# Pooled attention scores of two heads as one product over 128 rows, with zero-padded keys

## The chip, the cores and the metric

The kernel runs on one core of a Trainium2 chip. The metric is device time in microseconds (us) of one execution, from launch to end; less is better. A profile of one execution adds the span, which is the time from that execution's first instruction to its last, and the clock that TensorE was granted in each stretch: it has two levels, 2.4 GHz (shown as 1.00) and 1.2 GHz (0.50).

The engines are named as in the profile: PE is TensorE's matrix product, PEld its loading of weights (the stationary operand), DVE is VectorE, ACT is ScalarE, POOL is GpSimd, and SP is the engine that issues the DMAs.

## The reference, cut to what matters

Attention over 8 batches and 8 heads of 576 positions with 64 features, in two branches that are added, and then a gated feed-forward layer on all 4608 tokens:

```python
B, H, S, D = 8, 8, 576, 64; factor = 4; Sd = S // factor      # Sd = 144
q_d, k_d, v_d = (mean over 4 neighbouring positions)          # the pooled branch
out_d = sm_attn(q_d, k_d, v_d)                                # scores are 144 x 144 for each head
out_up = np.repeat(out_d, factor, axis=2)
mask = np.abs(pos[:, None] - pos[None, :]) < factor           # the local branch
out_local = softmax(where(mask, scale * q @ k.T, -1e9)) @ v
x = (out_up + out_local) as 4608 tokens x 512
gate = 1 / (1 + exp(-(x @ w_gate)));  val = x @ w_val         # 512 -> 1536
return (gate * val) @ w_out                                   # 1536 -> 512
```

The change is in the scores of the pooled branch, q_d @ k_d.T of each head.

## The kernel before, in words

**Units.** Attention is worked in 32 units. A unit is one batch and a pair of heads: head 0's 64 features lie on partitions 0 to 63, head 1's on partitions 64 to 127. Units 0 to 3 are batch 0, units 4 to 7 batch 1, and so on. Each unit is a dictionary of small steps (`unit_steps`, L412 on), and a table of positions says where in the program each step is written; the compile-time scheduler then fixes the order of the instructions on each engine from its own estimate of times. Each engine runs its own queue in order.

**The pooled branch of a unit.** `prep2` (L452) sums four neighbouring positions of q and k. They come as one tile `qkd` of 128 x 1152 from DRAM. `sum4` (L381) adds pairs in place on POOL (L383), then adds the two halves (L385) into the tile `qks` of 128 x 288: 144 columns of q sums and 144 of k sums, for both heads, one head on each half of the partitions. There is one buffer for `qks`. `s_down(h)` (L501) makes the scores of head h in one PSUM bank: two products of 64 rows (this head's partitions) x 72 query columns as weights, against 144 key columns, one for each half of the queries (qb). Then come the row maxima of both (L511, DVE, 72 x 288 read), their scaling (L512, ACT) and two exponentials with their sums (L514, ACT) into the tile `e`. `s_down(0)` is step d0, `s_down(1)` step d1; they are placed apart in the table. `norm_down` scales `e` into `ad`, `t_down` transposes it on PE (`adt`), and `av_down` multiplies by the pooled v (`od`): there `vdblk` holds both heads' v as a block-diagonal matrix with zeros beside it, so its products run over 128 rows.

**All products are issued at L394**, in `product`. One product of fp32 operands is two PE instructions in the profile (and two weight loads); one of fp16 is one. The weights' shape stands in the profile as rows*columns, "64*72" or "128*128", ahead of the shape of the moving operand.

**The local branch** uses `s` (scores of 10 blocks, block-diagonal q in `qblk`), `t` (softmax), `at` (transposes) and `x` (the product with v). For units 4 on, `s`, `sd`, `at`, `adt`, `od` and `x` share two PSUM banks by turns (L446, tile tag "att").

**The feed-forward part** goes by 9 chunks of 512 tokens and 12 blocks of 128 hidden features: `moe_gate` (products `pg`, 12 instructions), `moe_val` (`pv`, 12) and `moe_out` (`po`, 12), all fp16 in split high and low parts, 128*128 weights against 512 columns. During the first part of the program the weights arrive from DRAM, their maxima are taken (`hmx`), and they are converted (L205 to L215) on ACT, DVE and POOL. From position C1 on (L771 to L780), the steps of the later units are written between the blocks of `pg`, `pv` and `po` of chunks 1 to 8.

**At the start,** zeros are written into the block-diagonal tiles (`zeroed`, L98); `awake` products of a zero tile are put between the steps of the first units on PE.

Of the kernel before, what the change touches and what calls it, by code (L numbers as in the profile page):

```python
# [10 lines left out]
F32 = mybir.dt.float32  # L11
I32 = mybir.dt.int32
AF = mybir.ActivationFunctionType
ALU = mybir.AluOpType
AX = mybir.AxisListType
# [5 lines left out]
P = 128  # L21
# [9 lines left out]
SD = S // 4  # L31
QM = SD // 2
# [12 lines left out]
NWT = 1 + 2 * NPC  # L45
NST = 5
NPLAIN = 8
QKSCALE = 1.0 / 8
WAHEAD = 1
MAHEAD = 3  # L50
# [7 lines left out]
def attention_moe(ctx, tc, qk, qkd, v, vd, wg, wv, wo, mask, out):  # L58
    nc = tc.nc
# [3 lines left out]
    wk = ctx.enter_context(tc.tile_pool(name="wk", bufs=2))  # L63
# [34 lines left out]
    def zeroed(eng, shape, dtype, name):  # L98
        t = cp.tile(shape, dtype, tag=name, name=name)
        eng.memset(t, 0.0)  # L100
        return t

    def borrowed(eng, i, n):
        t = borrow(i, n * P)
        eng.memset(t, 0.0)
        return t.rearrange("p (a b) -> p a b", a=n)

    qblk = [zeroed(nc.vector, [P, 2 * NJ, P], F32, f"qblk{i}") for i in range(2)]
    vplain = [borrowed(nc.vector, 0, NBLK), borrowed(nc.gpsimd, 0, NBLK)]
    vdblk = [zeroed(nc.gpsimd, [P, NKC, P], F32, f"vdblk{i}") for i in range(2)]  # L110
    ad = zeroed(nc.gpsimd, [QM, 2, NKC, 2, WIN], F32, "ad")
    vblk = cp.tile([P, 2, NBLK, P], F16, tag="vblk", name="vblk")
    flat = {id(vblk): vblk.rearrange("p t b c -> p (t b c)").bitcast(F32)}
# [229 lines left out]
    qkraw, qkdraw, vdraw = {}, {}, {}  # L343
# [37 lines left out]
    def sum4(out, x, eng=nc.gpsimd):  # L381

        nc.gpsimd.tensor_tensor(out=x[:, :, 0:2], in0=x[:, :, 0:2], in1=x[:, :, 2:4], op=ALU.add)  # L383
        for ps, o in out:
            eng.tensor_tensor(out=o, in0=x[ps, :, 0], in1=x[ps, :, 1], op=ALU.add)  # L385

    ALL = slice(0, P)
    HALVES = [slice(0, 64), slice(64, P)]

    def product(o, w, x, first=True, last=True):  # L390

        pairs = ((0, 0), (0, 1), (1, 0)) if len(w) == 2 else ((0, 0),)
        for i, (a, c) in enumerate(pairs):
            nc.tensor.matmul(o, w[a], x[c], start=first and i == 0, stop=last and i == len(pairs) - 1)  # L394
# [4 lines left out]
    def own(t, u):  # L399
        owner[id(t)] = u  # L400

    def mine(t, u):
        assert owner[id(t)] == u, (owner[id(t)], u)

    def zero(*tiles):

        for t in tiles:
            nc.gpsimd.memset(flat[id(t)], 0.0)
            own(t, "zero")

    def unit_steps(u):
        b, hp = divmod(u, NPAIR)  # L412
        s = st[u] = {}
        NQ = 2 * NJ * R
        plain = u < NPLAIN
        AD = ad
# [8 lines left out]
        QB, VDB = qblk[u % 2], vdblk[u % 2]  # L425
# [3 lines left out]
        def take(t):  # L429
            if t is vblk and u in (NPAIR, NPLAIN):  # L430
                assert owner[id(t)] == "zero", (u, owner[id(t)])
            own(t, u)
# [13 lines left out]
        def bank(own, name):  # L446

            if u < NPAIR:
                return ps_o.tile([P, 512], F32, tag=own, name=name)
            return ps_a.tile([P, 512], F32, tag="att", name=name)  # L450

        def prep2():  # L452
            t = qkdraw[u]
            sums = wk.tile([P, 2, SD], F32, tag="qks", name=f"qks_{u}", bufs=1)
            sum4([(ALL, sums.rearrange("p a b -> p (a b)"))], t.rearrange("p (g f) -> p g f", f=4))
            s["qd"], s["kd"] = sums[:, 0], sums[:, 1]

        def s_local(j0, j1):
            mine(QB, u)
# [4 lines left out]
            if j0 == 0:  # L464
                s["t"] = wk.tile([P, NJ, 2 * WIN], F32, tag="t", name=f"t_{u}")
            nc.vector.scalar_tensor_tensor(  # L466
                out=s["t"][:, j0:j1, :], in0=pt[:, : n * 2 * WIN].rearrange("p (a b) -> p a b", a=n),
                scalar=QKSCALE, in1=mk[:, j0:j1, :], op0=ALU.mult, op1=ALU.add)

# [26 lines left out]
        def vdsum():  # L496
            take(VDB)
            x = vdraw[u].rearrange("p a b f -> p (a b) f")
            sum4([(ps, VDB[ps, :, ps]) for ps in HALVES], x, nc.vector if u in T["vd"] else nc.gpsimd)

        def s_down(h):  # L501
            pt = bank(f"o{h}", f"sd_{u}_{h}")
            hs = slice(h * 64, h * 64 + 64)
            for qb in range(2):
                o, rows = pt[:QM, qb * SD : (qb + 1) * SD], slice(qb * QM, (qb + 1) * QM)
                product(o, [s["qd"][hs, rows]], [s["kd"][hs]])
            if h == 0:
                s["e"] = wk.tile([QM, 2, 2, SD], F32, tag="e", name=f"e_{u}", bufs=1)
                s["sme"] = wk.tile([QM, 4], F32, tag="sme", name=f"sme_{u}")
            mx = wk.tile([QM, 2], F32, tag="mxd", name=f"mxd_{u}_{h}")  # L510
            nc.vector.tensor_reduce(mx, pt[:QM, : 2 * SD].rearrange("p (q c) -> p q c", q=2), axis=AX.X, op=ALU.max)  # L511
            nc.scalar.activation(mx, mx, AF.Copy, scale=-QKSCALE / 16)  # L512
            for qb in range(2):
                nc.scalar.activation(s["e"][:, qb, h, :], pt[:QM, qb * SD : (qb + 1) * SD], AF.Exp,  # L514
                                     bias=mx[:, qb : qb + 1], scale=QKSCALE / 16,
                                     accum_out=s["sme"][:, 2 * qb + h : 2 * qb + h + 1])

        def norm_down():
# [51 lines left out]
        def av_local(i0, i1):  # L570
            mine(VT, u)
            pt = bank("gate" if i0 == 0 else "val", f"x_{u}_{i0}")
            for i in range(i0, i1):
                product(pt[:, (i - i0) * R : (i - i0 + 1) * R], [x[:, i] for x in VBp], [x[:, i] for x in s["at"]])
            if i0 == 0:
                s["xs"] = wk.tile([P, S], F32, tag="xs", name=f"xs_{u}", bufs=1)
            t0, t1 = i0 * R, min(i1 * R, S)
            g0, g1 = t0 // 4, t1 // 4
            o = s["xs"][:, t0:t1].rearrange("p (g f) -> p g f", f=4)
            x = pt[:, : t1 - t0].rearrange("p (g f) -> p g f", f=4)  # L580
            y = s["od"][:, g0:g1].unsqueeze(2).to_broadcast([P, g1 - g0, 4])
            if plain:
                nc.vector.scalar_tensor_tensor(out=o, in0=x, scalar=sxb[:, b : b + 1], in1=y, op0=ALU.mult, op1=ALU.add)
            else:
                nc.vector.tensor_tensor(out=o, in0=x, in1=y, op=ALU.add)

        def xsplit():
            for c, o, i, n in segs_of_batch(b):
                x = xtile(c)
                src = s["xs"][:, i : i + n]  # L590
                nc.scalar.copy(x[:, hp, 0, o : o + n], src)  # L591
                eng = nc.vector if u in T["xd"] else nc.gpsimd
                eng.tensor_tensor(out=x[:, hp, 1, o : o + n], in0=src, in1=x[:, hp, 0, o : o + n], op=ALU.subtract)  # L593
            del st[u]
            done.add(u)

        return dict(
            prep0=lambda: None, prep1=prep1, prep2=prep2, s0=p1, s1=p2, sm=p2b,
            d0=lambda: s_down(0), d1=lambda: s_down(1), dn=norm_down,
            vd=vdsum, v=plain_v if plain else vsplit,  # L600
            a0=lambda: t_local(0, 3), a1=lambda: t_local(3, 5), at=t_down, od=av_down,
            x=lambda: (av_local(0, 8), av_local(8, 10), xsplit()),
# [7 lines left out]
    def moe_gate(c, fc):  # L610
        assert ("g", fc) in done
        assert all(u in done for u in range(min(NU, -(-(c + 1) * CH // S) * NPAIR))), (c, fc)
        x = xT[c]
        pt = ps_o.tile([P, CH], F32, tag="gate", name=f"pg_{c}_{fc}")
        for k in range(4):
            product(pt, [wg16[:, fc, a, k, :] for a in range(2)], [x[:, k, e, :] for e in range(2)], k == 0, k == 3)
        t = wk.tile([P, CH], F32, tag="tanh", name=f"tanh_{c}_{fc}")
        for b, o, n in segs_of_chunk(c):
            nc.scalar.activation(t[:, o : o + n], pt[:, o : o + n], AF.Tanh, scale=tsc[:, b, fc : fc + 1])  # L619
        return t  # L620
# [50 lines left out]
    def add(pos, f):  # L671
        steps.setdefault(pos, []).append(f)
# [31 lines left out]
    def base(u):  # L704
        if u < NPAIR:
            return 1 + u * T["pro"]
        if u < 2 * NPAIR:
            return T[f"u{u}"]
        if u < 3 * NPAIR:
            return C1 - T["b8"] + (u - 2 * NPAIR) * T["s8"]  # L710
        return C1 + T["b12"] + (u - 3 * NPAIR) * T["s12"]

    def offset(u, k):
        if u < NPAIR:
            return ALONE[k] * T["al"]
        return AMONG[k] * (T["am"] if u < 2 * NPAIR else 1)

    for u in range(NU):
        b, hp = divmod(u, NPAIR)
# [28 lines left out]
    add(T["z"], lambda: zero(vblk))  # L748
    add(base(NPLAIN - 1) + offset(NPLAIN - 1, "x") + 1, lambda: zero(vblk))

# [21 lines left out]
    for c in range(1, NCHUNK):  # L772
        for fc in range(NFC):
            t = moe_gate(c, fc)
# [86 lines left out]
```

## Time and profile before

| what | value |
|---|---|
| median of three runs | 1137.96 us (1137.18 to 1144.3) |
| the profiled execution, its own time | 1139.3 us |
| its span, first to last instruction | 1137.5 us |
| time outside the span | 1.8 us |
| mean granted TensorE clock | 0.968 |
| PE busy | 1097.7 us (96%) |
| DVE, ACT, POOL busy | 566.8, 488.1, 335.5 us |

A busy time is the sum of the durations of an engine's instructions without overlap. Durations of products on PE contain a tail that overlaps the next one, so the cost of a product in a stream is read from the distance between starts. In a timeline row the first number is the start in the span, the second the time from the first start to the last end of the merged instructions. "Idle before <- X" names what released an engine after a wait. The chain is the work that ended last, followed back from the end.

### The profile page before, as it was taken

The numbers are of one execution on the slowest core, as the hardware profiler recorded it, in microseconds if no ns is written. First come the engines' busy times: TensorE is split into PE (matmuls) and PEld (weight loads), VectorE is DVE, ScalarE is ACT, GpSimd is POOL, SyncE is SP. The second block draws the span as 40 slices with busy tenths as digits, with TensorE's granted clock in tenths as the row PEclk, the third lists the DMA queues.
The fourth block names the chain that finished last, engine by engine and source line by source line (L and its number), as shares of the span: only waits on it lengthen the run. The fifth ranks groups of instructions, "written<-read, shape, count | busy, mean of one in ns | idle before, by whom it ended". The sixth has DMA issues, their size and how long they took to land.

```text
span 1137.5 us, 16128 instructions
## 1 busy us (share of the span) xinstructions
PE 1097.7 (96%) x6319; PEld 603.6 (53%) x6319; DVE 566.8 (50%) x1048; ACT 488.1 (43%) x1112; POOL 335.5 (29%) x352
## 2 busy tenths in 40 slices
PE   7879879999999999999999999999999999999998
PEld 5854534555555555555555555555555554444443
DVE  7789989854445544444444444444444432122121
ACT  6635666533445444444445443544454332112112
POOL 6335646222223333333333332333243210000000
PEclk9758889999999999999999999999999999999999
DMA  9887766332213222132223121311121000000001
GB/s 361 330 311 258 252 210 216 118 100 86 70 47 131 60 65 70 59 111 74 69 69 106 61 65 56 119 59 54 48 94 36 1 1 37 1 1 37 1 1 37
DMA packets 31900, 110.33 MB, mean 97 GB/s; under 512 B 3536, under 2 KB 3664, under 8 KB 31824
## 3 DMA queue, kind: packets, MB, share of 16 engines
q1 hardware_dynamic: 31824, 109.30, 28.7%
q8 instruction: 50, 0.82, 0.3%
q14 instruction: 26, 0.21, 0.1%
HBM read 99.84 MB, written 9.44 MB: 96 GB/s over the span
## 4 chain that ended last, share of the span: by engine, by line
PE 86%; DVE 7%; DMA 2%; ACT 2%; issue 1%; POOL 1%; SPq 0%; DVEq 0%; ACTq 0%; POOLq 0%
PE po L394 24%; PE pg L394 23%; PE pv L394 23%; PE s L394 5%; PE x L394 3%; PE sd L394 3%; PE od L394 2%; PE at L546 1%; PE adt L556 1%; DVE wrg L207 1%; DMA v<-in_v_dram 1%; DVE vdblk L385 1%; DVE hmx L152 0%; DMA wo3c<-in_wo_dram 0%; DVE wrv L207 0%
## 5 line engine op out<-in xcount | busy, mean ns | idle before, releaser
L394 PE MATMUL pg<-xT,wg 128*128 128x512 f16 x1296 | 311.9, 383 | 6.7 <-ACT wg L214 3.5
L394 PE MATMUL pv<-xT,wv 128*128 128x512 f16 x1296 | 311.8, 381 | 0.1
L394 PE MATMUL po<-g,wo 128*128 128x512 f16 x1188 | 280.8, 379 | 0.0
L394 PEld LDWEIGHTS <-wg 128*128 128x128 f16 x1296 | 125.8, 99 | 152.0 <-issue 7.7
L394 PEld LDWEIGHTS <-wo 128*128 128x128 f16 x1296 | 124.7, 99 | 153.1 <-issue 8.2
L394 PEld LDWEIGHTS <-wv 128*128 128x128 f16 x1296 | 125.6, 99 | 141.0 <-issue 4.9
L627 DVE SCALAR_TENSOR_TENSOR tanh<-tanh,pv 128x512 f32<-128x512 f32 x108 | 73.8, 683 | 203.6 <-PE pv L394 199.3
L619 ACT ACTIVATE tanh<-pg,tsc 128x512 f32<-128x512 f32 (+7 forms) x192 | 87.0, 497 | 163.7 <-PE pg L394 163.7
L635 ACT ACTIVATE g<-tanh,gs 128x512 f16<-128x512 f32 x99 | 71.5, 723 | 149.6 <-DVE tanh L627 148.4
L636 DVE SCALAR_TENSOR_TENSOR g<-tanh,gs,g 128x512 f16<-128x512 f32 x99 | 88.6, 895 | 52.4 <-ACT g L635 51.9
L478 POOL TENSOR_TENSOR t<-t,mx 128x640 f32<-128x640 f32 x32 | 44.0, 1376 | 186.5 <-DVE mx L477 186.5
L394 PEld LDWEIGHTS s<-qk,qblk 128*128 128x128 f32 x600 | 77.9, 198 | 10.6 <-DVE hx L191 1.9
L394 PE MATMUL s<-qk,qblk 128*128 128x64 f32 x600 | 77.1, 279 | 2.6 <-DVE hx L191 1.4
L593 POOL TENSOR_TENSOR xT<-xs,xT 128x384 f16<-128x384 f32 (+7 forms) x58 | 53.1, 928 | 74.1 <-ACT xT L591 73.7
L488 POOL TENSOR_TENSOR t<-t,sm 128x640 f32<-128x640 f32 x28 | 36.8, 1316 | 96.0 <-DVE sm L486 94.6
L484 DVE TENSOR_REDUCE sm<-t 128x10 f32<-128x640 f32 x32 | 26.1, 817 | 66.1 <-ACT t L479 66.0
L156 ACT ACTIVATE vblk<-v,svb 64x640 f16<-64x640 f32 x48 | 39.7, 827 | 34.6 <-PE x L394 32.9
L466 DVE SCALAR_TENSOR_TENSOR t<-s,mk 128x384 f32<-128x384 f32 x64 | 31.0, 486 | 41.9 <-PE s L394 41.8
L438 ACT COPY qblk<-qk 64x580 f32<-64x580 f32 x60 | 40.5, 676 | 23.2 <-DMA qk<-in_qk_dram 19.5
L157 DVE SCALAR_TENSOR_TENSOR vblk<-v,svb,vblk 64x640 f16<-64x640 f32 x48 | 47.3, 985 | 3.2 <-ACT vblk L156 1.6
L512 ACT ACTIVATE mxd<-mxd 72x2 f32<-72x2 f32 x64 | 13.0, 203 | 83.5 <-DVE mxd L511 83.2
L383 POOL TENSOR_TENSOR qkd<-qkd 128x576 f32<-128x576 f32 x29 | 40.1, 1382 | 28.9 <-DMA qkd<-in_qkd_dram 28.5
(292 smaller groups left out, 1180.3 us busy)
## 6 DMA issues: line engine op xcount, KB each, us to landing
qk<-in_qk_dram SPq DMA_DIRECT2D x30, 610.0 KB, 3.8
qkd<-in_qkd_dram SPq DMA_DIRECT2D x29, 576.0 KB, 3.8
vd<-in_vd_dram SPq DMA_DIRECT2D x29, 384.0 KB, 3.5
v<-in_v_dram SPq DMA_DIRECT2D x32, 320.0 KB, 3.0
out_dram<-osb SPq DMA_DIRECT2D x16, 512.0 KB, 3.1
wo<-in_qk_dram SPq DMA_DIRECT2D x2, 610.0 KB, 10.5
wo<-in_qkd_dram SPq DMA_DIRECT2D x2, 576.0 KB, 9.3
out_dram<-osb SPq DMA_DIRECT2D x4, 256.0 KB, 2.3
```

The costliest lines, as they stand in the source:

```text
L156: nc.scalar.activation(hi, src, AF.Copy, scale=sc)
L157: nc.vector.scalar_tensor_tensor(out=lo, in0=src, scalar=sc, in1=hi, op0=ALU.mult, op1=ALU.subtract)
L383: nc.gpsimd.tensor_tensor(out=x[:, :, 0:2], in0=x[:, :, 0:2], in1=x[:, :, 2:4], op=ALU.add)
L394: nc.tensor.matmul(o, w[a], x[c], start=first and i == 0, stop=last and i == len(pairs) - 1)
L438: nc.scalar.copy(QB[ps, :, ps.start : ps.start + R], q_[ps])
L478: nc.gpsimd.tensor_tensor(out=t, in0=t, in1=mx.unsqueeze(2).to_broadcast([P, NBLK, WIN]), op=ALU.subtract)
L488: eng.tensor_tensor(out=t, in0=t, in1=sm.unsqueeze(2).to_broadcast([P, NBLK, WIN]), op=ALU.mult)
L593: eng.tensor_tensor(out=x[:, hp, 1, o : o + n], in0=src, in1=x[:, hp, 0, o : o + n], op=ALU.subtract)
L619: nc.scalar.activation(t[:, o : o + n], pt[:, o : o + n], AF.Tanh, scale=tsc[:, b, fc : fc + 1])
L627: nc.vector.scalar_tensor_tensor(out=t, in0=t, scalar=1.0, in1=pt, op0=ALU.add, op1=ALU.mult)
L635: nc.scalar.activation(g[:, 0], t, AF.Copy, scale=gs[:, fc : fc + 1])
L636: nc.vector.scalar_tensor_tensor(out=g[:, 1], in0=t, scalar=gs[:, fc : fc + 1], in1=g[:, 0], op0=ALU.mult, op1=ALU.subtract)
```

## The change

The pooled k of the two heads now goes into a tile `kdblk` of 128 x 2 x 144 that was zeroed at the start: head 0's sums fill partitions 0 to 63 of its first 144 columns, head 1's fill partitions 64 to 127 of the second 144, and the other two quarters stay zero. There are two such tiles, used by turns. One product of 128 rows x 72 query columns (both heads' q) against these 288 columns gives the scores of both heads for half of the queries. So `s_down` is called for a half of the queries instead of for a head, and makes one product of 288 columns where it made two of 144; the maxima, the exponentials and `e` keep their sizes and counts. `sum4` on POOL writes its second sum in three pieces instead of one: q (128 x 144) and k of each head (64 x 144 each). `qks` now holds q alone.

```diff
+NKD = 2
...
+    kdblk = [zeroed(nc.vector, [P, 2, SD], F32, f"kdblk{i}") for i in range(NKD)]
...
-        for ps, o in out:
-            eng.tensor_tensor(out=o, in0=x[ps, :, 0], in1=x[ps, :, 1], op=ALU.add)
+        for ps, o, g in out:
+            eng.tensor_tensor(out=o, in0=x[ps, g, 0], in1=x[ps, g, 1], op=ALU.add)
...
         def prep2():
-            t = qkdraw[u]
-            sums = wk.tile([P, 2, SD], F32, tag="qks", name=f"qks_{u}", bufs=1)
-            sum4([(ALL, sums.rearrange("p a b -> p (a b)"))], t.rearrange("p (g f) -> p g f", f=4))
-            s["qd"], s["kd"] = sums[:, 0], sums[:, 1]
+            x = qkdraw[u].rearrange("p (g f) -> p g f", f=4)
+            s["qd"] = wk.tile([P, SD], F32, tag="qks", name=f"qks_{u}", bufs=1)
+            s["kd"] = kdblk[u % len(kdblk)]
+            own(s["kd"], u)
+            sum4([(ALL, s["qd"], slice(0, SD))] + [(ps, s["kd"][ps, h], slice(SD, 2 * SD)) for h, ps in enumerate(HALVES)], x)
...
-        def s_down(h):
-            pt = bank(f"o{h}", f"sd_{u}_{h}")
-            hs = slice(h * 64, h * 64 + 64)
-            for qb in range(2):
-                o, rows = pt[:QM, qb * SD : (qb + 1) * SD], slice(qb * QM, (qb + 1) * QM)
-                product(o, [s["qd"][hs, rows]], [s["kd"][hs]])
-            if h == 0:
+        def s_down(qb):
+            mine(s["kd"], u)
+            pt = bank(f"o{qb}", f"sd_{u}_{qb}")
+            product(pt[:QM, : 2 * SD], [s["qd"][:, qb * QM : (qb + 1) * QM]], [s["kd"].rearrange("p h c -> p (h c)")])
+            if qb == 0:
...
-            for qb in range(2):
-                nc.scalar.activation(s["e"][:, qb, h, :], pt[:QM, qb * SD : (qb + 1) * SD], AF.Exp,
-                                     bias=mx[:, qb : qb + 1], scale=QKSCALE / 16,
+            for h in range(2):
+                nc.scalar.activation(s["e"][:, qb, h, :], pt[:QM, h * SD : (h + 1) * SD], AF.Exp,
+                                     bias=mx[:, h : h + 1], scale=QKSCALE / 16,
```

The scheduler's order changes with it. Three places follow. A name such as sd_31_1 is the tile of unit 31 and step d1 (the last number is only a counter), "72x144 x2" two products with an output of 72 x 144, and po_6_3 is a product of chunk 6 into its fourth output quarter; line numbers after the change are two or three higher.

The first place is PE in the middle of the program, at step d1 of unit 31, among the products of chunk 6; first before, then now:

```order
L394 MATMUL po_6_3_8139<-g_6_6_8510,wo16_111 128x512
L394 MATMUL sd_31_1_8203<-qks_31_7946 72x144 x2
L394 LDWEIGHTS wo16_111
L394 MATMUL po_6_3_8139<-g_6_6_8510,wo16_111 128x512
L394 LDWEIGHTS wo16_111
L394 MATMUL po_6_3_8139<-g_6_6_8510,wo16_111 128x512
L394 MATMUL od_30_8223<-adt16_30_8184,vdblk0_118 128x144 x3
```

```order
L396 MATMUL po_6_3_8144<-g_6_6_8514,wo16_111 128x512
L396 MATMUL sd_31_1_8208<-kdblk1_124,qks_31_7950 72x288
L396 LDWEIGHTS wo16_111
L396 MATMUL po_6_3_8144<-g_6_6_8514,wo16_111 128x512
L396 LDWEIGHTS wo16_111
L396 MATMUL po_6_3_8144<-g_6_6_8514,wo16_111 128x512
L396 LDWEIGHTS wg16_109
```

The two products of 144 columns have become one of 288 at the same place between `po` products, and od_30 stands a few products later.

The second place is PE near the start, where the pooled scores of unit 3 (sd_3) stood among the local products of units 0 to 2; first before, then now:

```order
L546 MATMUL at_0_0_280<-ident_103,t_0_178 128x128 x3
L394 MATMUL sd_3_0_614<-qks_3_468 72x144 x2
L394 MATMUL sd_3_1_631<-qks_3_468 72x144 x2
L130 MATMUL mxt1_266<-mxg1_270,ones_125 128x1
L546 MATMUL at_0_3_307<-ident_103,t_0_178 128x128 x2
L394 MATMUL x_0_0_447<-at16_0_284,wg16_109 128x58 x6
L556 MATMUL adt_2_582<-ident_103,ad_122 128x72 x6
L394 MATMUL s_2_0_368<-wo16_111,qblk0_112 128x64 x6
```

```order
L396 MATMUL s_2_3_389<-wo16_111,qblk0_112 128x64 x4
L396 MATMUL x_0_0_453<-at16_0_290,wg16_109 128x58 x2
L396 MATMUL x_0_8_464<-at16_0_290,wg16_109 128x58 x2
L396 MATMUL od_1_519<-adt16_1_451,vdblk1_120 128x144 x3
L547 MATMUL at_1_0_407<-ident_103,t_1_250 128x128 x3
L557 MATMUL adt_2_588<-ident_103,ad_126 128x72 x4
L547 MATMUL at_1_3_431<-ident_103,t_1_250 128x128 x2
L557 MATMUL adt_2_588<-ident_103,ad_126 128x72
L396 MATMUL sd_3_0_620<-kdblk1_124,qks_3_474 72x288
L396 MATMUL sd_3_1_636<-kdblk1_124,qks_3_474 72x288
```

sd_3 now stands behind s_2, x_0, od_1 and at_1 (and before the products x_1), where it stood ahead of all of them.

The third place is POOL at units 9 and 10; first before, then now:

```order
L385 TENSOR_TENSOR qks_9_2218<-qkd9_2105 128x288
L531 TENSOR_TENSOR ad_122<-e_8_2187,sme_8_2188 72x2x3x48 x2
L383 TENSOR_TENSOR qkd10_2223<-qkd10_2223 128x288x2
L478 TENSOR_TENSOR t_9_2258<-t_9_2258,mx_9_2283 128x640
L385 TENSOR_TENSOR qks_10_2367<-qkd10_2223 128x288
```

```order
L387 TENSOR_TENSOR qks_9_2223<-qkd9_2111 128x144
L385 TENSOR_TENSOR qkd10_2230<-qkd10_2230 128x288x2
L532 TENSOR_TENSOR ad_126<-e_8_2192,sme_8_2193 72x2x3x48 x2
L387 TENSOR_TENSOR kdblk0_122<-qkd10_2230 64x144 x2
L481 TENSOR_TENSOR t_9_2264<-t_9_2264,mx_9_2289 128x640
L387 TENSOR_TENSOR qks_10_2372<-qkd10_2230 128x144
```

The two pieces of k stand ahead of POOL's work on t_9, and only the q piece, which writes the single `qks` buffer, stands where the whole sum stood.

## Rows read from the trace of the kernel before

**Rows 1.** Stretches: length, busy us of PE, PEld, DVE, ACT, POOL; clock, DMA share, GB/s.

```profile
0.00:80.00 80.00, 63.20 (x370) 52.90 (x370) 61.01 (x126) 43.38 (x116) 36.52 (x45) 0.74 0.88 332
80.00:200.00 120.00, 102.95 (x486) 52.80 (x484) 114.57 (x202) 73.97 (x145) 69.98 (x48) 0.89 0.73 238
200.00:225.00 25.00, 24.49 (x127) 13.26 (x128) 22.01 (x38) 13.09 (x27) 6.96 (x8) 0.93 0.40 130
225.00:937.00 712.00, 711.08 (x4433) 396.02 (x4432) 329.63 (x628) 314.48 (x751) 221.26 (x252) 1.00 0.22 68
937.00:1137.50 200.50, 195.97 (x908) 88.65 (x906) 39.63 (x56) 43.18 (x78) 0.78 (x1) 1.00 0.04 16
```

**Rows 2.** The chain from 225 us to the end, by line.

```profile
by line: PE po L394 28.3%; PE pg L394 27.3%; PE pv L394 27.3%; PE s L394 5.5%; PE sd L394 3.3%; PE x L394 2.4%; PE od L394 2.1%; PE at L546 1.5%; PE adt L556 1.0%; PE mxt L130 0.2%; DVE xs L585 0.1%; DVE vblk L157 0.1%; DVE tsc L308 0.1%; A
```

**Rows 3.** Instructions of tile sd between 225 and 937 us: min/median/max ns.

```profile
L394 PE MATMUL sd<-qks x192: 282/283/340, 242.6 to 908.0; 64*72 64x144 f32 x192
```

**Rows 4.** Timeline of PE around one pooled-score step: start, us, what, count.

```profile
906.38 1.24 PE L394 MATMUL po<-g,wo 128*128 128x512 f16 x5
907.55 0.71 PE L394 MATMUL sd<-qks 64*72 64x144 f32 x4
908.19 0.60 PE L394 MATMUL po<-g,wo 128*128 128x512 f16 x2
908.63 0.90 PE L394 MATMUL od<-adt,vdblk 128*128 128x144 f32 x6
909.37 0.38 PE L394 MATMUL pg<-xT,wg 128*128 128x512 f16 x1
```

**Rows 5.** Timeline of PE around products with one weight column, and with one row.

```profile
815.22 0.81 PE L394 MATMUL pv<-xT,wv 128*128 128x512 f16 x3
815.87 0.27 PE L125 MATMUL mxt<-ident,vm 128*1 128x128 f32 x1
815.98 0.81 PE L394 MATMUL po<-g,wo 128*128 128x512 f16 x3
...
157.23 0.59 PE L394 MATMUL pv<-xT,wv 128*128 128x512 f16 x2
157.75 0.38 PE L130 MATMUL mxt<-mxg,ones 1*128 1x1 f32 x2
```

**Rows 6.** Timeline of PE near the start, units 0 to 4.

```profile
30.86 1.25 PE L394 MATMUL sd<-qks 64*72 64x144 f32 x8
...
43.71 1.13 PE L546 MATMUL at<-ident,t 128*128 128x128 f32 x5
...
50.10 0.90 PE L394 MATMUL od<-adt,vdblk 128*128 128x144 f32 x6
...
75.03 1.23 PE L394 MATMUL sd<-qks 64*72 64x144 f32 x4
```

**Rows 7.** Clock in the stretches of the first and last row of rows 6.

```profile
30.00:32.00 2.00, 2.00 (x12) 1.33 (x11) 1.17 (x5) 1.94 (x9) 0.00 (x0) 0.50 1.01 408
75.00:77.00 2.00, 1.26 (x5) 0.79 (x4) 2.00 (x5) 0.77 (x1) 0.00 (x0) 0.50 0.93 313
```

**Rows 8.** Sums at L385 between 225 and 937 us: min/median/max ns.

```profile
L385 POOL TENSOR_TENSOR vdblk<-vd x42: 522/530/984, 303.8 to 883.2; 64x192 f32<-64x192 f32 x42
...
L385 POOL TENSOR_TENSOR qks<-qkd x23: 700/707/1598, 251.3 to 879.2; 128x288 f32<-128x288 f32 x23
```

**Rows 9.** POOL's waits, 225 to 937 us: total us, times, longest.

```profile
POOL qks L385 <- PE sd L394: 75.5, 22, 8.7
```

**Rows 10.** Timeline of DVE: the last large memset, the first v, unit 3's output.

```profile
3.89 1.12 DVE L105 MEMSET wg<- 128x1280 f32 x1 [0.21 <-issue]
...
8.82 0.82 DVE L152 TENSOR_REDUCE vm<-v 128x1 f32<-128x640 f32 x1 [3.79 <-DMA v<-in_v_dram]
...
71.72 0.70 DVE L583 SCALAR_TENSOR_TENSOR xs<-x,sxb,od 128x464 f32<-128x464 f32 x1 [3.65 <-PE x L394]
```

**Rows 11.** PE's longest wait from 200 us to the end: total us, times, longest.

```profile
PE x L394 <- ACT e L514: 2.4, 1, 2.4
```

More of the change, by code (lines that the diff above doesn't have):

```diff
@@ L498, in vdsum @@
             x = vdraw[u].rearrange("p a b f -> p (a b) f")
-            sum4([(ps, VDB[ps, :, ps]) for ps in HALVES], x, nc.vector if u in T["vd"] else nc.gpsimd)
-        def s_down(h):
-            pt = bank(f"o{h}", f"sd_{u}_{h}")
-            hs = slice(h * 64, h * 64 + 64)
-            for qb in range(2):
-                o, rows = pt[:QM, qb * SD : (qb + 1) * SD], slice(qb * QM, (qb + 1) * QM)
-                product(o, [s["qd"][hs, rows]], [s["kd"][hs]])
-            if h == 0:
+            sum4([(ps, VDB[ps, :, ps], slice(None)) for ps in HALVES], x, nc.vector if u in T["vd"] else nc.gpsimd)
+        def s_down(qb):
[3 more added lines that the diff above has]
+            if qb == 0:
                 s["e"] = wk.tile([QM, 2, 2, SD], F32, tag="e", name=f"e_{u}", bufs=1)
                 s["sme"] = wk.tile([QM, 4], F32, tag="sme", name=f"sme_{u}")
-            mx = wk.tile([QM, 2], F32, tag="mxd", name=f"mxd_{u}_{h}")
-            nc.vector.tensor_reduce(mx, pt[:QM, : 2 * SD].rearrange("p (q c) -> p q c", q=2), axis=AX.X, op=ALU.max)
+            mx = wk.tile([QM, 2], F32, tag="mxd", name=f"mxd_{u}_{qb}")
+            nc.vector.tensor_reduce(mx, pt[:QM, : 2 * SD].rearrange("p (h c) -> p h c", h=2), axis=AX.X, op=ALU.max)
             nc.scalar.activation(mx, mx, AF.Copy, scale=-QKSCALE / 16)
-            for qb in range(2):
-                nc.scalar.activation(s["e"][:, qb, h, :], pt[:QM, qb * SD : (qb + 1) * SD], AF.Exp,
-                                     bias=mx[:, qb : qb + 1], scale=QKSCALE / 16,
+            for h in range(2):
+                nc.scalar.activation(s["e"][:, qb, h, :], pt[:QM, h * SD : (h + 1) * SD], AF.Exp,
+                                     bias=mx[:, h : h + 1], scale=QKSCALE / 16,
                                      accum_out=s["sme"][:, 2 * qb + h : 2 * qb + h + 1])
```

## The prediction

> **What bounds the kernel now.** I read the stretches first, then the chain, then the timeline of PE around one pooled-score step. The stretches show three stages [rows 1]. Up to 200 us PE is not the bound: in the 120 us from 80 to 200, DVE is busy for 114.57 us and PE for 102.95, at a mean granted clock of 0.89. From 200 us on PE is full, and from 225 to 937 us it is busy for 711.08 of 712 us at the full 2.4 GHz, while DVE, ACT and POOL have 329.63, 314.48 and 221.26 us of work there. So in that stretch a microsecond less on PE ends the kernel a microsecond earlier, and nothing that the other engines gain or lose in it counts until it makes PE wait. The chain from 225 us on says the same: it is PE almost throughout, and the pooled scores (sd) hold 3.3% of its 912.5 us, 30 us [rows 2]. Units 8 to 31 fall into this stretch: 192 sd instructions, four to a step, so 48 steps [rows 3].
>
> One step's true cost stands in the timeline [rows 4]. A product of 512 columns takes 0.65 / 3 = 0.217 us from start to start (pv, the first two rows of [rows 5]). Five of them from 906.38 should give PE to sd at 907.46; sd starts at 907.55. That is 0.09 us of gap at the entry. The four sd instructions hold PE from 907.55 to 908.19, 0.64 us. The od products have the same 144 columns in fp32, but 128 rows, and stand close: six from 908.63 to 909.37, 0.123 us each. At that pace four sd instructions would take 0.49. So a step holds PE for 0.73 us, and 0.24 of that is gap: 0.09 ahead of it, 0.15 inside it and behind it. The od group right behind has none.
>
> **The change part by part.** *The products.* The same number of columns passes: four instructions of 144 before, two of 288 now. At od's pace a step takes 2 x 0.246 = 0.49 us. The question is whether the gaps go too. Two things set sd apart from od: 64 rows instead of 128, and 72 weight columns instead of 128. The trace separates them [rows 5]. A product with 128 rows and one weight column (mxt<-ident,vm) follows three pv at 815.87, just when they are done, and the next po starts 0.11 us later: no gap on either side. A product with one row and 128 weight columns (mxt<-mxg,ones) starts 0.52 us after the first of two pv that need 0.43: the same 0.09 of gap as sd. So the gap goes with the rows, and with 128 rows I expect none. Each step saves 0.24 us (0.25 if the rounding of the rows falls the other way), and 48 steps save 11.5 to 12.0; I take 11.7. If the gaps stayed whole, the step would cost 0.73 as now and the saving is zero; that is the lower end.
>
> The Trainium skill, "TensorEngine Tiling (Array Packing)", section "Key Properties", says that changing the tiling mode drains TensorE. The trace agrees with it, with 0.09 us at a switch to few rows, and by that rule too the change removes both switches of a step.
>
> *What is given up.* Heads on different halves of the rows can run side by side, and the trace shows it once: at 30.86 both steps of unit 3 stand together, and their eight instructions take 1.25 us, while at 75.03 four of unit 4 alone take 1.23 [rows 6], both at 1.2 GHz [rows 7]. With 128 rows that is over: four instructions of 288 columns at half clock are 2 x 0.98 = 1.96 us, 0.7 more, for unit 3, and about half of that for unit 0, whose two steps also stand together, at full clock. From unit 8 on the two steps of a unit stand apart, four instructions at a time, so nothing is lost there.
>
> The Trainium skill, "TensorE: Matmul & The Clock Gate", section "Part 3: Packing small matmuls — row/col tiling", speaks against this change: it advises to keep small-row products in distinct row groups, since they run concurrently. The row at 30.86 agrees, but the steps that decide the end never stand together, so by that rule only the 1 us of units 0 and 3 would be lost.
>
> *POOL's sums.* One sum of 128x288 (0.707 us) becomes one of 128x144 and two of 64x144; a 64x192 one takes 0.530 [rows 8]. A piece of 144 columns lies between half of the whole sum, 0.35, and the whole, 0.71; I take 0.44, by the 64x192 row less a quarter of its columns and some fixed part. Three make 1.3 us: 0.6 more per unit, between 0.35 and 1.4. It can't be a gain, since the three pieces cover the same columns. From 225 us on that is 24 x 0.6 = 14 us more on an engine with 490 us to spare there. Does a step wait for it? Today it is POOL that waits for PE: 75.5 us in 22 waits for sd to free the single buffer of qks [rows 9]. In the new order only the q piece stands behind that wait, so what follows it is shorter than now (0.44 against 0.71). If the cover failed, PE would wait 0.6 us in each of 24 units, 14 us, all of the gain.
>
> *Maxima and exponentials* keep their shapes and counts: nothing. *Memsets:* two of 128x288 on DVE, under 0.3 us each by the 1.12 us of 128x1280, lie in the 3.79 us in which DVE waits for the first v [rows 10]: nothing.
>
> *The first 225 us.* PE has slack here, so its savings (12 steps that stand alone) don't count by themselves. POOL's 0.6 us more in 8 units is 4.8 us at most if each held up a full DVE; the lost pairing is 1 us. On the other side, PE reaches s_2 earlier, because sd_3 and most of adt_2 no longer stand ahead of it: 1.25 us and some more at half clock. And x waits 2.4 us for an exponential at about 200 us [rows 11], of which the earlier place of the last maxima of unit 7 may save a part. I take zero for this stretch, with 4.5 us either way.
>
> *Sum.* The profiled execution took 1139.3 us, 1.8 of it outside the span; 1139.3 - 11.7 = 1127.6. It was 1.3 above the median of the runs, so against the median: 1137.96 - 11.7 = 1126.3. The 200 us after 937 us have no sd and don't change.
>
> **The rivals.** *The gaps stay*, because they belong to a narrow fp32 weight load and not to the rows. For it: the load keeps 72 columns and fp32. Against it: the one-column fp32 product without a gap. Then the time is 1138, and with half of the gaps 1132.
>
> *The start gives part of it back.* The scheduler has rearranged every engine there. If DVE's full stretch ends 4.5 to 11 us later, the time is 1131 to 1137.
>
> *The start costs more than the products gain: slower.* The place is unit 3. DVE waits 3.65 us for x_3 and adds its od at 71.72 [rows 10], and the conversion of the weights queues behind that addition. The sd_3 products move from 30.86 to behind at_1, which ends at 44.8 [rows 6], 14 us later. In the trace od_3 follows sd_3 by 50.10 - 30.86 = 19.2 us, so it would come at about 64, still 7 us ahead of its use. If the steps between (maxima, exponentials, scaling, transposes, each behind other work on its engine) take longer than that, the excess moves the rest of the program. From 11.7 us of excess on the kernel is slower; 23 us of it, three times the spare time, give 1149.
>
> *The start gains:* if x_0, x_1 and the conversions behind them all move up, up to 5 us or more go as well: 1121.
>
> **How the numbers follow.** The forecast, gaps gone and the start within 4.5 us: 0.80, from 1122 to 1131. Gaps that stay in large part: 0.06. The start gives back 4.5 to 11: 0.08. Slower: 0.03. The start gains more: 0.03. I predict 1126.3. The range for 8 times in 10, taking in the bounds of the start, is 1121.5 to 1131.5. About 1% is what a measurement can tell from no change; 1% faster is 1126.6, just beside my forecast. So half of the 0.80 and a little more lies on that side, and the gaining start: faster 0.52. Of the slower rival some 0.02 reaches 1149; the rest, 0.46, is within 1%.
>
> **What would show it.** Right: sd stands as 128*72 with 288 columns, two instructions a step, about 0.49 us from the first start to the next product; the product ahead of it keeps 0.217; the share of sd in the chain after 225 us falls from 30 to about 23 us; PE is still full there; the pure stretch of pg, pv and po starts about 11.7 us earlier. The start is right if PE's full stretch begins at 200 us again. Wrong: a step of 0.7 us (gaps stay), PE waits for POOL's sums (cover gone), or PE's full stretch beginning more than 5 us from 200 us.

## The result and the profile after

Four runs of the changed kernel have a median of 1126.56 us (1125.82 to 1131.24); four runs of the kernel before have 1137.67. The measured ratio is 0.9891, with a 95% interval from 0.9864 to 0.9917; the medians alone give 0.9902, which lies inside it. So the change gains 11.1 us by the medians, and between 9.4 and 15.5 us by the interval; 1126.3 us was predicted. The profiled execution took 1126.46 us, its span is 1124.7 us, at a mean granted clock of 0.972.

The stretches of the changed kernel, with the columns of [rows 1]:

```profile
0.00:80.00 80.00, 62.32 (x350) 52.05 (x350) 60.23 (x125) 42.05 (x110) 39.34 (x56) 0.74 0.86 324
80.00:200.00 120.00, 98.55 (x475) 49.59 (x476) 114.08 (x207) 75.08 (x153) 68.77 (x55) 0.93 0.72 246
200.00:225.00 25.00, 25.00 (x136) 13.64 (x134) 22.86 (x36) 13.16 (x25) 10.60 (x11) 0.96 0.33 120
225.00:937.00 712.00, 710.23 (x4386) 393.93 (x4385) 332.99 (x630) 315.76 (x755) 238.01 (x296) 1.00 0.21 68
937.00:1124.70 187.70, 183.12 (x849) 82.81 (x847) 37.56 (x54) 40.65 (x73) 0.00 (x0) 1.00 0.05 17
```

Nothing in the fourth row looks faster: PE is full, as in [rows 1], at the same clock. The gain appears as work that has moved forward, out of the last stretch, which is 187.70 us long instead of 200.50: the last step of sd starts at 894.86 us, where it started at 907.55 [rows 4]. In such a stage PE's busy time says nothing about whether its work is well packed; the distances between starts do. POOL's busy time in the fourth row has grown by 16.8 us.

The chain from 225 us on, by line (to set beside [rows 2]):

```profile
by line: PE po L396 28.0%; PE pg L396 27.5%; PE pv L396 27.4%; PE s L396 5.5%; PE sd L396 2.6%; PE x L396 2.4%; PE od L396 2.0%; PE at L547 1.5%; PE adt L557 1.0%; DVE vblk L159 0.4%; DMA v<-in_v_dram 0.3%; ACT vblk L158 0.2%; PE mxt L132 0
```

The share of sd is 2.6% of 899.7 us, 23.4 us, where it was 30.

One pooled-score step in the timeline of PE (to set beside [rows 4]; start, us, what, count):

```profile
576.14 2.11 PE L396 MATMUL pg<-xT,wg 128*128 128x512 f16 x9
578.09 0.65 PE L396 MATMUL sd<-kdblk,qks 128*72 128x288 f32 x2
578.57 2.54 PE L396 MATMUL pv<-xT,wv 128*128 128x512 f16 x11
```

Nine pg products from 576.14 at 0.216 us end their turn at 578.08; sd starts at 578.09, so there is no gap at the entry. The pv behind it starts 0.48 us later (0.49 and 0.50 us at two other steps). A step of the kernel before held PE for 0.73 us.

PE's waits of the changed kernel from 200 us to the end (total us, times, longest):

```profile
PE at L547 <- DVE t L469: 0.7, 1, 0.7
PE s L396 <- DVE t L469: 0.6, 1, 0.6
PE x L396 <- DVE xs L586: 0.4, 1, 0.4
```

No wait is for POOL's sums. The 2.4 us of [rows 11] is not in this list because that wait now ends at 197.20 us, ahead of the window, and has become 1.29 us; its row stands further down.

The sums of one unit on POOL, by shape (min/median/max ns; to set beside [rows 8]):

```profile
L387 POOL TENSOR_TENSOR qks<-qkd x29: 439/447/1353, 8.6 to 867.6; 128x144 f32<-128x144 f32 x29
...
L387 POOL TENSOR_TENSOR kdblk<-qkd x58: 432/446/2187, 9.0 to 847.6; 64x144 f32<-64x144 f32 x58
```

### The profile page after: what moved, and what is told of

Same layout as the page of the kernel before. It is cut to its first block, busy times and chain, and to the rows that moved or that the text cites. A ratio compares the mean times of both kernels' runs of the same rounds, so it can differ in the third digit from the quotient of the medians.

```text
span 1124.7 us, 15921 instructions
## 1 busy us (share of the span) xinstructions
PE 1079.2 (96%) x6191; PEld 592.0 (53%) x6191; DVE 567.7 (50%) x1050; ACT 486.7 (43%) x1112; POOL 356.7 (32%) x416
## 4 chain that ended last, share of the span: by engine, by line
PE 85%; DVE 8%; ACT 2%; DMA 2%; issue 2%; POOL 1%; DVEq 0%; POOLq 0%; SPq 0%; ACTq 0%
PE po L396 24%; PE pg L396 23%; PE pv L396 23%; PE s L396 5%; PE x L396 3%; PE sd L396 2%; PE od L396 2%; PE at L547 1%; PE adt L557 1%; DVE vdblk L387 1%; DVE hmx L154 1%; DVE wrg L210 1%; DMA wg6c<-in_wg_dram 1%; DVE wrv L209 0%; DVE wrg L209 0%
## 5 line engine op out<-in xcount | busy, mean ns | idle before, releaser
L515 ACT ACTIVATE e<-sd,mxd 72x144 f32<-72x144 f32 x128 | 47.0, 370 | 2.4
```

What stands on the lines that cost most here:

```text
L515: nc.scalar.activation(s["e"][:, qb, h, :], pt[:QM, h * SD : (h + 1) * SD], AF.Exp, bias=mx[:, h : h + 1], scale=QKSCALE / 16, accum_out=s ...
```

## The experiments

Two theories stood against each other for the products. A: the gap belongs to products over 64 rows, whatever their number and columns. B: it belongs to the number of instructions, or to narrow fp32 weights (72 columns), so that the change gained by halving the count. The first two runs separate them; the third asks what the 64 rows could have given if the heads' products had been laid side by side; the fourth doubles the cost that the change adds on POOL. The rest deals with a loss that the first three brought to light. Apart from the first result, every experiment was timed beside the kernel before on its own chip, whose median was 1139.5 us each time and not 1137.67; so kernels of different groups are compared by their ratios to it as well as by their medians.

**Four products over 128 rows.** The changed kernel, with a step's product cut into one for each head:

```diff
-            product(pt[:QM, : 2 * SD], [s["qd"][:, qb * QM : (qb + 1) * QM]], [s["kd"].rearrange("p h c -> p (h c)")])
+            for h in range(2):
+                product(pt[:QM, h * SD : (h + 1) * SD], [s["qd"][:, qb * QM : (qb + 1) * QM]], [s["kd"][:, h]])
```

> The change, but with two products of 144 columns a step as before the change, each over 128 rows against one head's zero-padded keys: four products and four fp32 weight loads of 72 columns a step in the profile, as before, only the rows differ. Theory (the gap goes with the 64 rows): no gap ahead of or behind a step, four sd instructions from start to start 0.123 us each, 0.49 us a step, and the time of the changed kernel, 1126.6 us within 2. Rival (the gap goes with narrow fp32 weights, or the saving with fewer products and loads): the gaps of 0.09 and 0.15 us stay, 0.73 us a step, about 1138 us.

Measured: 1132.8 us median (1129.08 to 1134.12, ten runs), ratio 0.9931 (0.991 to 0.9951). That is neither the theory's time (within 2 us of 1126.6) nor the rival's (about 1138).

**The sums alone.** Padded sums, and the four 64-row products of the kernel before:

```diff
-        def s_down(qb):
+        def s_down(h):
...
+            hs = slice(h * 64, h * 64 + 64)
+            for qb in range(2):
+                o, rows = pt[:QM, qb * SD : (qb + 1) * SD], slice(qb * QM, (qb + 1) * QM)
+                product(o, [s["qd"][hs, rows]], [s["kd"][hs, h]])
```

> The change's sums on POOL and its padded key tiles, but the products as before, 64 rows of one head against 144 columns of its quarter. Theory (the saving is PE's gaps after 225 us; sums are hidden; the start moves by a few us at most): steps of 0.73 us with their gaps, and 1138 us within 4, the difference being that of the start. Rival (the changed order or sums give the saving): about 1127 us. If the sums cost as much as their 0.6 us a unit, up to 14 us more than before, 1152 us.

Measured: 1145.34 us median (1142.22 to 1148.82, ten runs), ratio 1.0045 (1.0024 to 1.0067). This lies 3 us above the theory's range (1134 to 1142) and far from the rival's 1127; no wait of PE from 200 us on names a sum here either.

Both times missed, so the steps themselves have to decide. A step of the first of the two in the timeline of PE:

```profile
899.77 0.81 PE L396 MATMUL po<-g,wo 128*128 128x512 f16 x3
900.42 0.65 PE L396 MATMUL sd<-kdblk,qks 128*72 128x144 f32 x4
900.91 0.59 PE L396 MATMUL po<-g,wo 128*128 128x512 f16 x2
```

And one of the second:

```profile
908.77 2.32 PE L396 MATMUL po<-g,wo 128*128 128x512 f16 x10
911.02 0.71 PE L396 MATMUL sd<-kdblk,qks 64*72 64x144 f32 x4
911.66 0.60 PE L396 MATMUL po<-g,wo 128*128 128x512 f16 x2
```

Both kernels have four instructions of 144 columns behind fp32 weights of 72 columns. With 128 rows three po products take their 0.65 us, sd follows at once and holds PE for 0.49 us. With 64 rows, ten po products should end at 908.77 + 2.16 = 910.93; sd starts at 911.02, 0.09 us later, and then takes 0.64. The two kernels run the same sums, and both have the stall that is told of below: at the same place PE waits 1.5 and 0.6 us in the first, 1.3 and 0.6 us in the second, and both then have 0.51 from 356 to 366 us. Their medians differ by 12.5 us, where 48 steps at 0.24 to 0.25 us make 11.5 to 12.0. Theory A holds, B falls: the rows carry the gain, and the halved count of instructions adds nothing that can be seen in a step (0.49 us with four instructions, 0.48 to 0.50 with two).

The Trainium skill, "TensorEngine Tiling (Array Packing)", section "Key Properties", has it that a change of the tiling mode drains TensorE. These two timelines agree, at 0.09 us for the entry to the 64-row products; no run here shows the drain itself.

But both are some 5 to 6 us slower than the kernel whose products they share in cost: 1132.8 against 1126.56 of the changed kernel (4.8 us by the ratios), 1145.34 against 1139.54 of the kernel before on the same chip. PE's waits of the first one between 340 and 370 us show where:

```profile
PE mxt L127 <- ACT od L569: 1.5, 1, 1.5
PE mxt L132 <- DVE mxg L131: 0.6, 1, 0.6
```

Right behind them PE's clock falls, as the stretches show:

```profile
350.00:356.00 6.00, 3.85 (x23) 2.47 (x21) 2.55 (x9) 5.79 (x15) 3.25 (x4) 1.00 0.60 222
356.00:366.00 10.00, 9.31 (x61) 7.59 (x61) 5.71 (x17) 4.82 (x13) 6.15 (x8) 0.51 0.42 156
```

PE is idle for 2.15 of 6 us and is then granted 0.51 for 10 us, which costs about 5 us of work. The timelines tell why. At this place chunk 1 ends, and the rest of chunk 2 needs `x` of unit 11 (x_11). In the changed kernel od_11 stands well ahead of x_11, with other products between:

```profile
350.48 0.90 PE L396 MATMUL od<-adt,vdblk 128*128 128x144 f32 x6
351.21 0.65 PE L396 MATMUL sd<-kdblk,qks 128*72 128x288 f32 x2
351.69 1.67 PE L396 MATMUL pv<-xT,wv 128*128 128x512 f16 x7
353.21 2.75 PE L396 MATMUL po<-g,wo 128*128 128x512 f16 x12
355.80 0.27 PE L127 MATMUL mxt<-ident,vm 128*1 128x128 f32 x1
355.90 0.81 PE L396 MATMUL x<-at,vblk 128*128 128x58 f16 x24
```

In the kernel with four products the scheduler had used up pv and po by then:

```profile
349.23 2.75 PE L396 MATMUL po<-g,wo 128*128 128x512 f16 x12
351.81 0.90 PE L396 MATMUL od<-adt,vdblk 128*128 128x144 f32 x6
352.55 0.65 PE L396 MATMUL sd<-kdblk,qks 128*72 128x144 f32 x4
354.68 0.27 PE L127 MATMUL mxt<-ident,vm 128*1 128x128 f32 x1 [1.47 <-ACT od L569]
```

Only one sd step, 0.49 us, lies between od_11 and what needs its result.

**Pairs.** The kernel before, with both heads' 64-row products in one block of eight on two PSUM banks. From unit 8 on a small product of zeros into each bank stands ahead of the block, so that the eight stay together:

```diff
+            gates = [nc.tensor.matmul(s["pt"][h][:, :1], idle[:, :P], idle[:, :1], start=True, stop=True) for h in range(2)]
...
+                for qb in range(2):
+                    for h, hs in enumerate(HALVES):
+                        o, rows = s["pt"][h][:QM, qb * SD : (qb + 1) * SD], slice(qb * QM, (qb + 1) * QM)
+                        product(o, [s["qd"][hs, rows]], [s["kd"][hs]])
```

> The kernel before, with both heads' products of a unit issued as one block of four, head by head in turn, in two PSUM banks; from unit 8 on a product of one column of zeros into each bank holds the block back until both banks are free, so that its eight instructions stand together. Theory (64 rows cost a gap at each switch, but two heads on different row halves run side by side): a block takes about 0.65 us and 0.09 ahead of it where two steps took 1.46 before and 0.97 take in the changed kernel; with about 0.06 for the two small products 0.80 a unit, 24 units save 24 x 0.66 = 16 us against before: 1122 us, 4 below the changed kernel, if waiting for two banks makes PE wait nowhere. Rival (they don't run side by side, or PE waits for the banks): 0.98 and one pair of gaps a unit, 1132 us, or later by the waits.

Measured: 1129.12 us median (1128.58 to 1130.6, four runs), ratio 0.9906 (0.9871 to 0.994), where the theory had 1122. One block in the timeline of PE:

```profile
574.01 1.24 PE L394 MATMUL po<-g,wo 128*128 128x512 f16 x5
575.09 0.17 PE L506 MATMUL sd<-idle 128*128 128x1 bf16 x1
575.18 0.71 PE L394 MATMUL sd<-qks 64*72 64x144 f32 x8
575.83 1.69 PE L394 MATMUL po<-g,wo 128*128 128x512 f16 x7
```

Eight instructions take 0.65 us from start to next, about as long as four alone took in [rows 4], with 0.09 us ahead of them from the start of the small product: 0.74 us for a unit, against 0.97 for the changed kernel's two steps. The Trainium skill, "TensorE: Matmul & The Clock Gate", section "Part 3: Packing small matmuls — row/col tiling", says that such products run concurrently, and this row agrees.

By 0.74 against 0.97 us the pairs should beat the changed kernel by 24 x 0.23 = 5.5 us. They did not: PE waits 4.6 us at 351 us for an exponential, behind od_11 and the block of eight, and has 10 us at a clock of 0.51. And at four later chunk ends, from 478 to 831 us, PE waits 2.2 us for xs and 1.3 us for xT, 3.5 us in all, where the changed kernel's list above has 0.4 us for xs and nothing for xT. All four kernels with pairs have these waits, so they are part of what this form of the pairs costs.

**The key sums twice.** The changed kernel, writing the two 64x144 sums of k a second time:

```diff
-            ... + [(ps, s["kd"][ps, h], slice(SD, 2 * SD)) for h, ps in enumerate(HALVES)], x)
+            ... + [(ps, s["kd"][ps, h], slice(SD, 2 * SD)) for h, ps in enumerate(HALVES)] * 2, x)
```

> The change, with the two key pieces of each sum written twice (the same values): some 0.9 us more of POOL's work a unit, 29 us in all. Theory (POOL's sums are hidden behind a PE-bound stretch): 1126.6 us within 3, no wait of PE for POOL after 225 us. Rival (PE waits for the sums): up to 21 us more after 225 us, 1148 us.

Measured: 1127.71 us median (1125.34 to 1130.02, four runs), ratio 0.9891 (0.9854 to 0.9929), the same ratio as the changed kernel. Its main stretch and, below, PE's waits from 200 us on:

```profile
225.00:937.00 712.00, 711.02 (x4389) 393.87 (x4388) 334.61 (x634) 315.97 (x754) 263.87 (x341) 1.00 0.21 68
```

```profile
PE x L396 <- ACT od L568: 0.8, 1, 0.8
PE sd L396 <- DVE xs L586: 0.6, 1, 0.6
PE pg L396 <- POOL xT L594: 0.3, 1, 0.3
```

POOL has another 25.9 us of work there (263.87 against 238.01), PE is as full as before, and no wait names a sum. One wait of 0.3 us, at 478 us, is for POOL's xT, where the expectation had no wait for POOL at all. The sums are hidden, with room for two more key pieces a unit.

**Units 8 to 11 earlier.** New theory: the kernel with four products loses its 6 to 8 us at the boundary of chunk 1 alone. A test that touches no product: the entry `b8` of the table of positions, which sets where units 8 to 11 are written, from 6.75 to 8.75.

```diff
-b8=6.75
+b8=8.75
```

For the kernel with four products over 128 rows:

> The kernel of e1 (two products of 144 columns over 128 rows in a step) with b8 8.75 in place of 6.75: the steps of units 8 to 11 stand two places earlier, so x_11 comes before PE has run out of the work of chunk 1. Theory (e1 loses about 3.5 us of waiting and 5 us of half clock at 353 us because PE is ahead there and waits for the chain of unit 11): no wait above 1 us and no stretch of clock 0.50 between 300 and 400 us; about 1132.8 - 8 = 1125. Rival (the wait goes somewhere else, since the other engines then have to carry units 8 to 11 sooner after their full start): PE waits 3 us or more in all between 225 and 330 us, and the time stays at 1131 to 1134.

Measured: 1125.89 us median (1124.3 to 1126.62, four runs), ratio 0.9875 (0.9859 to 0.989). Its stretches at the boundary:

```profile
350.00:356.00 6.00, 6.00 (x35) 3.48 (x34) 2.31 (x7) 4.13 (x11) 1.42 (x2) 1.00 0.33 100
356.00:366.00 10.00, 9.83 (x50) 4.93 (x48) 6.54 (x20) 7.91 (x19) 5.64 (x7) 1.00 0.53 169
```

The idle time and the half clock are gone, and with them 6.9 us, as the theory had it. So four products over 128 rows take no longer than the changed kernel's two of 288 columns.

For the changed kernel itself:

> The changed kernel with b8 8.75 in place of 6.75. Theory: it loses only about 1 us at the boundary of chunk 1, so there is little to win: 1124.5 to 1126.5. Rival (units 8 to 11 then crowd the start): 1128 or more, with PE waits of 2 us or more between 200 and 330 us.

Measured: 1130.04 us median (1128.48 to 1130.96, four runs), ratio 0.9912 (0.9896 to 0.9927). My theory missed; its rival had the time, though not the place. PE's waits from 200 us on come to 4.4 us, most of them behind 475 us and not between 200 and 330 us, and the clock between 200 and 225 us is 0.90.

And for the kernel before:

> The kernel before with b8 8.75 in place of 6.75, the control for the other two. Theory: like the changed kernel it has little to win there, 1136 to 1139, and the distance to the changed kernel with the same edit stays at about 11.7 us. Rival: the edit itself is worth several us to any version, 1133 or less.

Measured: 1146.36 us median (1140.42 to 1154.06, ten runs), ratio 1.005 (1.0025 to 1.0075). Both expectations missed. Here the loss lies at the end of chunk 2: PE waits 2.8 us at 483.6 us for DVE's `t`, and then has 6.8 us at a clock of 0.50. The same entry of the table is worth 6.9 us to one version and costs the kernel before 6.8. For the changed kernel the loss is 3.5 us by the medians and 2.4 by the ratios (0.9912 against 0.9891), whose intervals overlap, so it is less sure.

**Pairs with units 8 to 11 earlier** (`b8` 10.75):

> The kernel of e3 (both heads' 64-row products side by side, in blocks of eight) with b8 10.75 in place of 6.75. e3 waits some 8 us and has 10.2 us of half clock (5 us of work) around 352 us, though its sd work is the smallest of all. Theory (the boundary takes what the pairs save): without that wait and half clock it comes to 1119 to 1122, faster than the changed kernel. Rival (the pairs don't save PE time over the whole, or the wait moves on): 1126 to 1130.

Measured: 1128.47 us median, ratio 0.9898 (0.9845 to 0.9952). The four runs fall in two groups, 1122.39 and 1123.16, then 1133.79 and 1134.13: the first lies just above the theory's range, the second above the rival's, and the median between them says little. The profiled one is the fastest: PE is busy for 30.00 us of the 30 from 340 to 370, at full clock. It shows that the pairs can come to 1122 us; what the other two lost, and where, was not profiled and stays open.

**The change's start, pairs from unit 8 on.** The changed kernel up to unit 7, then sums without padding and the blocks of eight:

```diff
+            if u >= 2 * NPAIR:
+                sums = wk.tile([P, 2, SD], F32, tag="qks", name=f"qks_{u}", bufs=1)
...
+            if u >= 2 * NPAIR:
+                if qb == 0:
+                    s_pair()
+                return
```

> The changed kernel up to unit 7, and from unit 8 on the pairs of e3: sums of 128x288 without padding, both heads' 64-row products side by side in a block of eight. In e3 a block holds PE for 0.65 us and 0.09 of gap, 0.74 for a unit, against 0.97 for the changed kernel's two steps: 24 x 0.23 = 5.5 us less after 225 us. But unit 11's x stands last in the work of chunk 1, right behind its od, as in e3. Theory (PE's saving counts only as long as x_11 is not waited for): the pairs' 5.5 us come, and a wait of 3 to 6 us with 10 us of half clock (5 us of work) at 350 us takes them back: 1126 to 1132. Rival (the boundary costs only those that come to it 4 us early, as e1 and e3 did, and this start does not): 1120 to 1123.

Measured: 1135.37 us median (1131.78 to 1137.28, ten runs), ratio 0.996 (0.994 to 0.9979). PE's longest waits from 200 us on:

```profile
PE mxt L127 <- ACT e L531: 4.4, 1, 4.4
PE s L396 <- DVE xs L621: 2.2, 4, 0.6
```

The wait behind od_11 is there, at 357 us, without a start that is 4 us ahead: od_11 stands at 354.69 us here, 350.48 in the changed kernel and 348.81 in the first kernel with pairs. So the rival is out, and an early arrival is not what makes the wait. The time lies above my range too, by 3 us; the 4.2 us by which od_11 comes later than in the changed kernel were lost ahead of it (from 80 to 200 us its granted clock was 0.90, against 0.93), and why is not shown.

The same with `b8` 11.75:

> p1 with b8 11.75 in place of 6.75: units 8 to 11 stand five places earlier, so x_11 comes long before the end of chunk 1. Theory: no wait above 1 us and no half clock near 350 us, and the pairs' 5.5 us stay: 1120 to 1123, faster than the changed kernel. Rival (units 8 to 11 crowd the start, as in b2, where PE had done 2.7 us less by 225 us): 1124 to 1130, with the loss between 150 and 260 us.

Measured: 1130.06 us median (1127.36 to 1135.27, five runs), ratio 0.9928 (0.9893 to 0.9963). The wait at the boundary is gone, but the rival's time came: half clock for most of 242 to 249 us (0.53 over the seven). The waits for xs and xT at four chunk ends are there again, 3.5 us in all. The median of no version here beats the changed kernel beyond the spread of the runs.

## Why the prediction was right

**The bound.** PE's full stretch decided, as the prediction read from [rows 1, 2]. The span fell by 12.8 us between the two profiled executions, of which 48 steps at 0.24 to 0.25 us are 11.5 to 12.0.

**The gap belongs to the rows.** The prediction drew this from two products with one weight column and with one row [rows 5]. It is now shown by the pair of kernels that differ in it: 12.5 us between their medians, and 0.49 against 0.73 us for a step. The rival in which a narrow fp32 load keeps the gap is out, since that load was kept.

**POOL's sums.** Estimated at 0.44 us a piece and 1.3 us a unit, measured 0.447 + 2 x 0.446 = 1.34. They are hidden, and the kernel that writes the key sums twice shows by how much. POOL's wait for sd [rows 9] went from 75.5 to 70.9 us, so it is still POOL that waits for PE.

**Lost pairing.** The four instructions of 288 columns in the start, at half clock, were put at 1.96 us for unit 3. The timeline of PE near the start of the changed kernel has 1.92 from start to start for unit 2, at a granted clock of 0.50 (to set beside [rows 6]). Unit 3's own four, at 43.74, took 1.70 us at 0.56, as the next product on PE starts at 45.44:

```profile
24.89 2.13 PE L396 MATMUL sd<-kdblk,qks 128*72 128x288 f32 x4
26.81 0.93 PE L557 MATMUL adt<-ident,ad 72*128 72x72 f32 x6
...
43.74 1.86 PE L396 MATMUL sd<-kdblk,qks 128*72 128x288 f32 x4
...
54.73 1.00 PE L396 MATMUL od<-adt,vdblk 128*128 128x144 f32 x6
```

**Unit 3, the slower rival.** Its products moved to 43.74, about where the prediction had them (behind 44.8). But od_3 came 11.0 us behind, not 19.2, at 54.73 instead of 64. So the prediction was wrong to take the 19.2 us of the kernel before for the length of the chain: at least 8.2 of them were not needed. The addition of od_3 on DVE came at 73.64, against 71.72 in [rows 10], so the margin was 18 us and not 7.

**The start.** Zero within 4.5 us was predicted. With 11.7 us for the steps, about 1 us of the span is left for the start. The counts say the same: apart from sd, PE of the changed kernel has 3 po, 6 adt and 2 at fewer left at 225 us, an estimated 1.2 us by their distances in the rows above. PE's full stretch begins within the 5 us that the prediction allowed, and the wait ahead of it, 2.40 us in [rows 11], is 1.1 us shorter:

```profile
197.20 1.10 PE L396 MATMUL x<-at,vblk 128*128 128x58 f32 x4 [1.29 <-ACT e L515]
```

That shorter wait is the part that the prediction thought might be saved there. That zero was close is partly luck: the kernel with four products over 128 rows lies 6.9 us apart from itself by order alone.

**What the prediction did not see.** The order around x_11. The changed kernel kept 4.6 us of ready work (sd, pv, po) between od_11 and x_11; with nearly the same products, four experiments lost it, at a price of 6.9 us in the one where it was measured. That the change itself kept this order is luck, as far as the prediction goes. No part of the prediction speaks of this place, and a rival for it, worked out from the order at each chunk's end, would have belonged there.

## What to carry to other kernels

Where a full PE sets the end, look at the distances between starts around each short group of products: a group over fewer rows than its neighbours costs a gap on both sides, and zeros that fill the rows up remove it, if another engine has room to write them. Two such groups on different halves of the rows, side by side, take less still per unit (0.74 against 0.97 us here), but the gain has to survive the order around it, and in the medians here it did not. After any change to an order that a scheduler makes, look for places where a result is needed right behind the work that makes it: in the kernel with four products some 2 us of waiting cost 5 us more through the clock.

## What was not expected of the hardware

Waits of some 2 us in all on a PE that had been full were followed by about 10 us at 1.2 GHz in the kernel with four products (0.51 from 356 to 366 us above), and so were 4.6 us in the kernel with pairs (0.51 from 354.4 to 364.6 us). Elsewhere the fall was shorter: 6.8 us behind the 2.8 us of waiting in the kernel before with units 8 to 11 earlier, and only some 3 us (0.50 from 202 to 205 us) behind the 2.4 us of [rows 11]. The changed kernel's wait of 0.7 us was followed by none, while in the last experiment the fall at 242 us came behind waits of at most 0.5 us. So the length of one wait does not tell what the clock will take for it; what else decides is not shown here.

Two conversions on DVE took 0.88 and 0.89 us in the kernel before, where POOL stood idle from 479.25 to 482.07 us, and 5.71 us together (1.24 and 4.44) in that kernel with units 8 to 11 earlier. DVE before:

```profile
479.97 0.88 DVE L157 SCALAR_TENSOR_TENSOR vblk<-v,svb,vblk 64x640 f16<-64x640 f32 x1
...
481.14 0.89 DVE L157 SCALAR_TENSOR_TENSOR vblk<-v,svb,vblk 64x640 f16<-64x640 f32 x1
```

DVE and POOL with units 8 to 11 earlier:

```profile
480.06 5.71 DVE L157 SCALAR_TENSOR_TENSOR vblk<-v,svb,vblk 64x640 f16<-64x640 f32 x2
```

```profile
479.96 1.87 POOL L531 TENSOR_TENSOR ad<-e,sme 72x288 f32<-72x288 f32 x2 [1.00 <-DVE xs L585]
481.79 1.41 POOL L593 TENSOR_TENSOR xT<-xs,xT 128x320 f16<-128x320 f32 x2
483.17 1.14 POOL L383 TENSOR_TENSOR qkd<-qkd 128x576 f32<-128x576 f32 x1
```

POOL is busy beside them for nearly all of that time, and DVE's `t`, for which PE then waits, is queued behind them. That POOL's work is the cause was not tested by itself.
